# Sliding-window attention feeding a mixture of experts: reads of token rows ahead of weight loads and two groups ahead, constants and clearing spread over more attention units

## The chip, the cores and the metric

The kernel runs on one core of one Trainium2 chip. The metric is the device time of one execution in microseconds (us), a median of three runs. A core has five engines that work through their own instruction streams in order: TensorE (PE, matrix products; its weight loads are listed as PEld), VectorE (DVE), ScalarE (ACT), GpSimd (POOL) and SyncE (SP). SyncE does no arithmetic here: it issues nearly all loads, one after the other, and a load that must wait for something holds back every load behind it in the program. Sixteen DMA engines move the data.

## The reference

There are 4608 tokens (8 batches of 576) with 8 heads of 64. The first half is attention over a window of 128 positions with a bias that falls with the distance; the second half sends every token to the one of 8 experts whose logit is largest, and multiplies the expert's output by the softmax weight of that choice.

```python
def _attn_ref(q, k, v):                       # 8 batches, 8 heads, 576 positions, 64 per head
    scores = scale * np.matmul(q, k.transpose(0, 1, 3, 2))
    rel = pos[:, None] - pos[None, :]
    bias = slopes[:, None, None] * (-np.abs(rel).astype(np.float32))[None, :, :]
    mask = (rel >= 0) & (rel < 128)
    scores = np.where(mask, scores + bias[None], -1000000000.0)
    attn = softmax(scores)
    return np.matmul(attn, v)

def _moe_ref(x, w_gate, w1, w2):              # x: 4608 x 512; w1: 8 x 512 x 1024; w2: 8 x 1024 x 512
    logits = x @ w_gate
    expert_idx = np.argmax(logits, axis=1)
    gate_w = softmax(logits)[arange, expert_idx]
    for e in range(8):                        # tokens sorted by expert
        h = np.maximum(x_sorted[lo:hi] @ w1[e], 0.0)
        y_sorted[lo:hi] = h @ w2[e]
    return gate_w[:, None] * y_sorted[inv_perm]
```

(Softmax is written out in the original; it is shortened here.)

## The kernel before

**Attention.** The work is cut into 32 units (`NU`), one for each batch and pair of heads. Unit `u` computes scores on TensorE, exponentials on ScalarE, a product with a table of bias factors on VectorE (`factors`), and sums of overlapping blocks on GpSimd (`merge`, tile `mg`). TensorE then does `values` and `totals` of unit `u - 1`; `totals` reads `mg`. Once a batch is through, its gating is cut into "tasks" (logits, gate, rows, place, send), of which some are done in each later unit. A `send` scatters 128 finished rows of 514 numbers (512 values, the token's number, the gate weight) into the DRAM tensor `x_rows`, which holds a region for each expert. Each region's first 512 rows are cleared beforehand by `clear_rows`.

```python
later = [lambda: make_identity(nc, ident[:])]
def routing_constants():                        # all on GpSimd
    nc.gpsimd.memset(lt_strict[:], 1.0)
    nc.gpsimd.affine_select(lt_strict[:], lt_strict[:], compare_op=ALU.is_gt, ...)
    nc.gpsimd.memset(ones_sq[:], 1.0)
    ...                                         # zero_e, keep
later.append(routing_constants)

def iota(name, shape, pattern, base, mult, whole=False):
    t_i = consts.tile(shape, I32, name=name + "_i")
    later.append(lambda: nc.gpsimd.iota(t_i[:], ...))
    if whole:
        return t_i
    t_f = consts.tile(shape, F32, name=name)
    later.append(lambda: nc.gpsimd.tensor_copy(t_f[:], t_i[:]))
    return t_f
...                                             # first_w, region, thr, kx, tail, tok
        for u in range(NU + 1):
            b, hp = divmod(u, HP)
            slow = u < 7
            if u < NU:
                if u + HP < NU:
                    load_qk(u + HP)
                if hp == 1 and 1 < b + 1 < NB:
                    load_v(b + 1)
                if 0 < u <= E:
                    clear_rows(u - 1)
                ...
                scores(u)
                factors(u, 0)
            do(0 if slow else 1)                # so many tasks
            if u < NU:
                factors(u, 1)
                merge(u)
                if u + 1 < HP:
                    table(u + 1)
                if u == 2:
                    for make in later:
                        make()
                    start_routing()
            if u > 0:
                values(u - 1, 0)
                values(u - 1, 1)
                totals(u - 1)
                if hp == 0 and u < NU:
                    tasks += tasks_of(b - 1)
            do(0 if slow else 2 if len(tasks) < 14 else 3)
        do(len(tasks))
        last_tasks()
```

`last_tasks` does the gating of the last batch and, between its steps, the first 256 rows of expert 0 (`early`), whose outputs go through the attention's own tiles named `e` and are scattered to the output from there.

**Experts.** Fifteen groups follow: the other 256 rows of expert 0, then for each of experts 1 to 7 a full group of 512 rows, and after each of these a group of 128 rows (`x`) that did not fit. A full group is computed by a scheme of seven products for a 2x2 block product (`seven1`, `seven2`), the others plainly (`layer1`, `layer2`). `gather` reads a group's rows from `x_rows` into one of two `xg` buffers; `turn` transposes them on TensorE; `tokens` takes the row numbers out of `xg` for the scatter; the last step of a group scales its output by the gate weight, which it reads in `xg`.

```python
    def gather(g):
        n = g["n"]
        xg = g["xg"] = pools["x"].tile([P, NJ, RW], F32, name="xg")       # two buffers
        ...
            nc.sync.dma_start(xg[:, j0:j1, :], src[:, j0:j1, :])
    def layer2(g, j, ps, zo):
        ...
        nc.scalar.activation(zo, ps[:], AF.Copy, scale=g["xg"][:, j, Dm + 1 :])
        send_out(g, j, zo)
    ...
        g = groups[0]
        g["w1"], g["w2"] = expert_w.pop(0)      # loaded during attention
        get_w1(groups[1])
        gather(g)
        turn(g, range(g["n"]))
        for i, g in enumerate(groups):
            after = groups[i + 1 : i + 3] + [None, None]
            if after[0] is not None:
                gather(after[0])
                after[0]["w2"] = load_w2(after[0]["src"][1])
            ...                                 # layer 1: seven1 twice, or layer1
            tokens(g)
            if after[1] is not None:
                get_w1(after[1])
            if after[0] is not None:
                turn(after[0], range(after[0]["n"]))
                ...
            ...                                 # layer 2: seven2, or layer2
```

The pools of the expert stage are laid over those of attention, which are closed by then: `xg` (two buffers of 8 KB in each partition) falls on the buffers of k and v, and `weights1`, the second set of weight buffers, falls partly on the pool of `probs`, `e` and `mg`.

Of the kernel before, what the change touches and what calls it, by code (L numbers as in the profile page):

```python
# [21 lines left out]
def kernel(  # L22
# [47 lines left out]
    GT = KT + 1  # L70
    keep = consts.tile([P, E, GT + 1], F32, name="keep")

    def routing_constants():
        nc.gpsimd.memset(lt_strict[:], 1.0)
# [4 lines left out]
        nc.gpsimd.memset(ones_sq[:], 1.0)  # L79
        nc.gpsimd.memset(zero_e[:], 0.0)  # L80
        nc.gpsimd.memset(keep[:], 1.0)
        nc.gpsimd.memset(keep[:, :, 0:1], 0.0)

    later.append(routing_constants)

    def iota(name, shape, pattern, base, mult, whole=False):
        t_i = consts.tile(shape, I32, name=name + "_i")
        later.append(lambda: nc.gpsimd.iota(t_i[:], pattern=pattern, base=base, channel_multiplier=mult))
        if whole:
            return t_i  # L90
        t_f = consts.tile(shape, F32, name=name)
        later.append(lambda: nc.gpsimd.tensor_copy(t_f[:], t_i[:]))
        return t_f

    first_w = iota("first_w", [P, E], [[-1, E]], E, 0)
    region = iota("region", [P, E], [[N, E]], 0, 0)
# [17 lines left out]
    soon.append(lambda: nc.gpsimd.memset(zero_row[:], 0.0))  # L114
    soon.append(lambda: nc.gpsimd.memset(zero_row.bitcast(I32)[:, Dm : Dm + 1], 2 * N))

    def clear_rows(e):
        nc.sync.dma_start(
            x_d[e * N : e * N + CAP, :].rearrange("(j p) r -> p j r", p=P),
            zero_row[:, None, :].to_broadcast([P, NJ, RW]),  # L120
        )
# [59 lines left out]
            nc.vector.tensor_copy(early_n[:], rk[:, 0, GT:])  # L181

    def scatter(t, row):
        ins = nc.gpsimd.indirect_dma_start(  # L184
            out=x_d[:, :], out_offset=bass.IndirectOffsetOnAxis(ap=slots[:, t : t + 1], axis=0),
            in_=row, in_offset=None, bounds_check=E * N - 1, oob_is_err=False,
        )
        ins = getattr(ins, "ins", ins)
        tc.declare_no_dep(ins, group=f"rows_in{n_pass[0]}", reason="disjoint rows")
        tc.add_to_no_dep_group(f"rows_in{n_pass[0]}", ins)  # L190
# [239 lines left out]
            tc.add_to_no_dep_group(f"rows_out{n_pass[0]}", ins)  # L430

    def tokens(g):
        bits = g["xg"].bitcast(I32)[:, : g["n"], Dm]
        si = g["si"] = plain.tile([P, NJ], I32, name="si", bufs=2)[:, : g["n"]]
        if "mask" in g:
            nc.vector.tensor_tensor(si, bits, g["mask"][:, 0, :], op=ALU.bitwise_and)
            nc.vector.tensor_tensor(si, si, g["mask"][:, 1, :], op=ALU.bitwise_or)
        else:
            nc.vector.tensor_copy(si, bits)

    def turn(g, tiles, ps=None):

# [11 lines left out]
    def layer1(g, fb, ps):  # L454
        n = g["n"] * P
        if fb == 0:
            g["h"] = plain.tile([P, FB, EJ * P], F32, name="h2")
        for db in range(DB):
            nc.tensor.matmul(  # L459
                ps[:, :n], lhsT=g["w1"][:, db, fb * P : (fb + 1) * P], rhs=g["xT"][:, db, :n],  # L460
                start=(db == 0), stop=(db == DB - 1),
            )
        nc.scalar.activation(g["h"][:, fb, :n], ps[:, :n], AF.Relu)

    def layer2(g, j, ps, zo):
        for fb in range(FB):
            nc.tensor.matmul(  # L467
                ps[:], lhsT=g["h"][:, fb, j * P : (j + 1) * P], rhs=g["w2"][:, fb, :], start=(fb == 0),
                stop=(fb == FB - 1),
            )  # L470
        nc.scalar.activation(zo, ps[:], AF.Copy, scale=g["xg"][:, j, Dm + 1 :])  # L471
        send_out(g, j, zo)


# [22 lines left out]
    with tc.tile_pool(name="tab", bufs=1) as tab, \  # L497
# [257 lines left out]
        def last_tasks():  # L755
            g = early
            turns = [lambda j=j: turn(g, [j], sp_banks[j]) for j in range(EJ)]
            hid = [lambda fb=fb: layer1(g, fb, ps_m.tile([P, S - 2 * P], F32, name="m")) for fb in range(FB)]
            ts = tasks_of(NB - 1)
            more = {2: turns, 6: hid[:3], 8: hid[3:4], 9: hid[4:5], 10: hid[5:6], 11: hid[6:]}  # L760
            for i, task in enumerate(ts):
                task()
                for step in more.get(i + 1, ()):
                    step()
            extras(tab.tile([P, H, W // 2], F32, name="fac2").rearrange("p h c -> p (h c)"))
            tokens(g)
            for j in range(EJ):
                layer2(g, j, sp_banks[EJ + j], ex.tile([P, 2, W // 2], F32, name="e").rearrange("p a c -> p (a c)")[:, :Dm])

# [4 lines left out]
        load_v(1)  # L774
        tasks = []

        def do(n):
            for task in tasks[:n]:
                task()
            del tasks[:n]  # L780

        for u in range(NU + 1):
            b, hp = divmod(u, HP)

            slow = u < 7
            if u < NU:
                if u + HP < NU:
                    load_qk(u + HP)
                if hp == 1 and 1 < b + 1 < NB:
                    load_v(b + 1)  # L790
                if 0 < u <= E:
                    clear_rows(u - 1)
                if u == NU // 2:
                    expert_w[0] = load_w1(moe_w1[0]), load_w2(moe_w2[0])
                scores(u)
                factors(u, 0)
            do(0 if slow else 1)
            if u < NU:
                factors(u, 1)
                merge(u)  # L800
                if u + 1 < HP:
                    table(u + 1)
                if u == 2:
                    for make in later:
                        make()
                    start_routing()
            if u > 0:
                values(u - 1, 0)
                values(u - 1, 1)
                totals(u - 1)  # L810
                if hp == 0 and u < NU:
                    tasks += tasks_of(b - 1)
            do(0 if slow else 2 if len(tasks) < 14 else 3)
        do(len(tasks))
        last_tasks()

# [148 lines left out]
    def seven2(g, more):  # L965
# [17 lines left out]
        def weigh(th, dh, src):  # L983
            for i in range(2):
                j = 2 * th + i
                nc.scalar.activation(o[:, th, dh, i, :], src[:, i, :], AF.Copy, scale=g["xg"][:, j, Dm + 1 :])  # L986

        def post(n, ba, bb, bc):
            if n == 1:
# [56 lines left out]
    def experts(first):  # L1046
# [11 lines left out]
        if first:  # L1058
            g["w1"], g["w2"] = expert_w.pop(0)
        else:  # L1060
            get_w1(g)
        get_w1(groups[1])
        gather(g)
        if not first:
            g["w2"] = load_w2(g["src"][1])
            extras(pools["wk"].tile([P, FB, NJ * P], F32, name="h_sb").rearrange("p f n -> p (f n)"))
            run(w1_sums(g))
        turn(g, range(g["n"]))
        if not first:
            x_sums(g)  # L1070
        for i, g in enumerate(groups):
            after = groups[i + 1 : i + 3] + [None, None]
            full = [a for a in after if a is not None and a["n"] == NJ and "w1s" not in a]
            if after[0] is not None:
                gather(after[0])
                after[0]["w2"] = load_w2(after[0]["src"][1])
            if g["n"] == NJ:
                hidden(g)
                order = (1, 6, 7, 5, 2, 3, 4)
                ws = w2_sums(g)  # L1080
                seven1(g, 0, order, two_banks(3), temps(), {6: ws[:1], 7: ws[1:2], 5: ws[2:3], 3: ws[3:]})
# [8 lines left out]
            tokens(g)  # L1090
            if after[1] is not None:
                get_w1(after[1])
            if after[0] is not None:
                turn(after[0], range(after[0]["n"]))
                if after[0]["n"] == NJ:
                    x_sums(after[0])
            if i == 0 and first:
                count_in_range()
            if g["n"] == NJ:
                g["zo"] = pools["wk"].tile([P, NJ, Dm], F32, name="zo")  # L1100

                ws = w1_sums(full[0]) if full else []
# [8 lines left out]
    def plain_group(g):  # L1111
        get_w1(g)
        g["w2"] = load_w2(g["src"][1])
        gather(g)
        turn(g, range(g["n"]))
        for fb in range(FB):
            layer1(g, fb, bank(fb))
        tokens(g)
        plain_layer2(g)

    more = nc.values_load(n_more_i[0:1, 2:3], min_val=0, max_val=N * H + NX + EJ * P)
# [51 lines left out]
```

## Time and profile before

| | |
|---|---|
| time, median of 3 | 764.14 us (762.72 to 765.75) |
| span of the profiled execution | 763.8 us |
| TensorE busy | 704.8 us (92%) |
| VectorE busy | 368.6 us (48%) |
| ScalarE busy | 225.7 us (30%) |
| GpSimd busy | 184.2 us (24%) |
| DMA | 130.80 MB, mean 171 GB/s |

Attention with the gating of the last batch and the early rows of expert 0 ends near 247 us; the groups of experts run from there to about 752 us. "Busy" is the time in which an engine had an instruction under way. With TensorE busy for 92% of the span, the time that can be saved without changing the products lies in the remaining 8% and in the stretches in which its clock was low. A wait in the lists is written as "engine tile line <- what it waited for", then the sum in us, how many times, and the longest.

### The profile page before, as it was taken

Reading aid. Unit: us, or ns where it says so; the run is one execution under the profiler, and the core shown is the slowest. Engines: PE = TensorE matmul, PEld = TensorE weight load, DVE = VectorE, ACT = ScalarE, POOL = GpSimd, SP = SyncE. Lnnn points to the kernel's source line nnn. Section 1 sums busy time; section 2 is a strip of 40 time slices with the busy share of each in tenths; the row PEclk is TensorE's granted clock in tenths of the full one; section 3 lists DMA queues with packets and bytes.
Section 4 is the critical chain, followed back from the end, with each engine's and each line's share of the span. In section 5 each row is a group of like instructions: output and inputs, shape, how many; then the busy total and the mean of one; then the engine's idle time right before and its main releaser. Section 6 shows DMA issues by size and latency. Waiting matters only on the chain.

```text
span 763.8 us, 12630 instructions
## 1 busy us (share of the span) xinstructions
PE 704.8 (92%) x5158; PEld 566.2 (74%) x5158; DVE 368.6 (48%) x637; ACT 225.7 (30%) x538; POOL 184.2 (24%) x192
## 2 busy tenths in 40 slices
PE   5799899989999399999999999999999999999993
PEld 4576667667684277887888788788788978878891
DVE  8457677866654223532633544263453346235310
ACT  4555655545421021212213122221221213122120
POOL 5747766776541001011002001100200200020020
PEclk9899999989899599999999999999999999999997
DMA  9996668862121834209325720923663192275010
GB/s 335 371 374 214 213 225 314 257 188 91 54 84 42 315 111 151 98 27 332 112 111 178 288 110 28 340 94 111 221 246 110 54 359 64 95 280 189 1 56 7
DMA packets 54291, 130.80 MB, mean 171 GB/s; under 512 B 4175, under 2 KB 4175, under 8 KB 54224
## 3 DMA queue, kind: packets, MB, share of 16 engines
q1 hardware_dynamic: 47696, 110.97, 42.1%
q0 software_dynamic: 6000, 18.92, 6.5%
q8 instruction: 42, 0.69, 0.4%
q14 instruction: 25, 0.20, 0.1%
q10 hardware_dynamic: 528, 0.02, 0.0%
HBM read 102.55 MB, written 28.12 MB: 171 GB/s over the span
## 4 chain that ended last, share of the span: by engine, by line
PE 66%; issue 14%; DMA 6%; POOL 6%; DVE 5%; ACT 2%; SPq 0%; POOLq 0%; DVEq 0%
PE b L916 16%; PE a L916 11%; PE c L916 11%; PE a L467 5%; DMA xg<-x_rows 5%; PE m L625 5%; PE sp L580 5%; PE m L723 2%; PE sm L644 2%; POOL x_rows L184 2%; PE m L459 1%; PE a L459 1%; POOL mg L609 1%; DMA k_sb<-in_kT_dram 1%; POOL mg L606 1%
## 5 line engine op out<-in xcount | busy, mean ns | idle before, releaser
L422 POOL DMA_INDIRECT out_dram<-zo,si x28 | 29.5, 1053 | 326.1 <-ACT zo L986 321.8
L587 ACT ACTIVATE e<-sp 128x512 f32<-128x512 f32 x128 | 66.8, 600 | 44.7 <-PE sp L580 36.3
L606 POOL TENSOR_TENSOR mg<-probs 128x768 f32<-128x768 f32 x31 | 56.9, 1836 | 65.0 <-DVE probs L599 34.2
L625 PE MATMUL m<-probs,v_sb 128*64 128x256 f32 (+3 forms) x768 | 66.7, 322 | 1.2 <-DVE probs L594 0.8
L580 PE MATMUL sp<-q_sb,k_sb 64*64 64x192 f32 (+2 forms) x1152 | 57.1, 344 | 9.1 <-DMA k_sb<-in_kT_dram 9.0
L625 PEld LDWEIGHTS m<-probs,v_sb 128*64 128x64 f32 x768 | 49.9, 142 | 19.2 <-issue 4.7
L580 PEld LDWEIGHTS sp<-q_sb,k_sb 64*64 64x64 f32 x1152 | 48.5, 149 | 20.7 <-issue 9.8
L594 DVE TENSOR_TENSOR probs<-e,fac 128x1024 f32<-128x1024 f32 x32 | 40.5, 1267 | 42.0 <-ACT e L587 36.1
L467 PE MATMUL a<-w,h 128*128 128x512 f32 x128 | 56.3, 592 | 0.0
L986 ACT ACTIVATE zo<-zo,xg 128x256 f32<-128x256 f32 x42 | 19.1, 501 | 119.4 <-DVE zo L997 78.2
L916 PE MATMUL a<-xgT,w 128*128 128x256 f32 x224 | 53.0, 379 | 0.0
L916 PE MATMUL b<-xTs,w1s 128*128 128x256 f32 x224 | 52.9, 379 | 0.0
L916 PE MATMUL a<-w,h_sb 128*128 128x256 f32 x224 | 50.6, 379 | 0.0
L916 PE MATMUL b<-w2s,hs 128*128 128x256 f32 x224 | 50.6, 379 | 0.0
L916 PEld LDWEIGHTS a<-xgT,w 128*128 128x128 f32 x224 | 42.5, 190 | 8.7 <-issue 3.3
L184 POOL DMA_INDIRECT x_rows<-xs,slots x36 | 43.4, 1206 | 19.3 <-DVE xs L726 9.5
L916 PEld LDWEIGHTS b<-xTs,w1s 128*128 128x128 f32 x224 | 42.6, 190 | 5.8
L916 PEld LDWEIGHTS b<-w2s,hs 128*128 128x128 f32 x224 | 42.6, 190 | 5.8
L916 PEld LDWEIGHTS a<-w,h_sb 128*128 128x128 f32 x224 | 42.0, 190 | 5.4
L467 PEld LDWEIGHTS a<-w,h 128*128 128x128 f32 x128 | 23.7, 190 | 26.8 <-issue 26.8
L422 POOL DMA_INDIRECT out_dram<-zx,si x9 | 8.7, 972 | 139.7 <-ACT zx L471 139.7
L599 DVE TENSOR_TENSOR probs<-e,fac 128x1024 f32<-128x1024 f32 x32 | 40.5, 1264 | 2.0 <-ACT e L587 1.9
(212 smaller groups left out, 1178.2 us busy)
## 6 DMA issues: line engine op xcount, KB each, us to landing
w<-in_moe_w_dram SPq DMA_DIRECT2D x30, 2048.0 KB
q_sb<-in_qT_dram SPq DMA_DIRECT2D x32, 288.0 KB
k_sb<-in_kT_dram SPq DMA_DIRECT2D x32, 288.0 KB
x_rows<-zero_row SPq DMA_DIRECT2D x8, 1028.0 KB
xg<-x_rows SPq DMA_DIRECT2D x16, 514.0 KB
v_sb<-in_v_dram SPq DMA_DIRECT2D x8, 1024.0 KB
v_sb<-in_v_dram SPq DMA_DIRECT2D x8, 256.0 KB
xg<-x_rows SPq DMA_DIRECT2D x7, 257.0 KB
```

The source lines that it names most:

```text
L184: ins = nc.gpsimd.indirect_dma_start(out=x_d[:, :], out_offset=bass.IndirectOffsetOnAxis(ap=slots[:, t : t + 1], axis=0), in_=row, in_offs ...
L422: ins = nc.gpsimd.indirect_dma_start(out=out[:, :], out_offset=bass.IndirectOffsetOnAxis(ap=g["si"][:, j : j + 1], axis=0), in_=row, in_of ...
L459: nc.tensor.matmul(ps[:, :n], lhsT=g["w1"][:, db, fb * P : (fb + 1) * P], rhs=g["xT"][:, db, :n], start=(db == 0), stop=(db == DB - 1),)
L467: nc.tensor.matmul(ps[:], lhsT=g["h"][:, fb, j * P : (j + 1) * P], rhs=g["w2"][:, fb, :], start=(fb == 0), stop=(fb == FB - 1),)
L580: nc.tensor.matmul(sps[s][par][part * HALF : (part + 1) * HALF, c : c + n], lhsT=k_sb[u][half, k0 : k0 + HALF], rhs=q_sb[u][half, q0 : q0 ...
L587: nc.scalar.activation(exps[u][s][:, par, :], sps[s][par][:], AF.Exp, scale=D ** -0.5)
L594: nc.vector.tensor_tensor(to.rearrange("p a (j c) -> p a j c", c=2 * P), e.rearrange("p a (j c) -> p a j c", c=2 * P), fac[:, heads, None, ...
L599: nc.vector.tensor_tensor(to, e[:], fac2[:, heads, :], op=ALU.mult)
L606: eng.tensor_add(mg[:, :, : 3 * P].rearrange("p a (t c) -> p a t c", c=P), two[:, :, :, 0, :], two[:, :, :, 1, :],)
L625: nc.tensor.matmul(xp[par * HALF : (par + 1) * HALF, lo - q0 : hi - q0], lhsT=v_sb[b][:, j, h * D : (h + 1) * D], rhs=probs[u][:, par, c + ...
L916: nc.tensor.matmul(out_of[:, i, :], lhsT=lhs(i, k), rhs=rhs(k), start=(first and i == 0 and k == 0), stop=(k == nk - 1), skip_group_check= ...
L986: nc.scalar.activation(o[:, th, dh, i, :], src[:, i, :], AF.Copy, scale=g["xg"][:, j, Dm + 1 :])
```

## The change

It has four parts. (1) In the expert stage the rows of the first two groups are read ahead of the weight load that used to stand first on SyncE. (2) The rows of every further group are read two groups ahead instead of one; for that, `tokens` copies the gate weights into a small tile `gw` of their own as well, right after `turn`, so that an `xg` buffer is free once its rows are transposed and not only after the group's last product. (3) The constants for the routing are made in six portions, one in each of units 0 to 5 (the rest in unit 6), with the fills and conversions on VectorE and only the iotas and selects on GpSimd. (4) The eight clearings go to units 1, 2, 3, 4, 6, 7, 8 and 10 instead of 1 to 8; the tasks begin in unit 9 instead of 7, with up to four at the second place of a unit when 20 or more stand in line.

```diff
+    later += [
+        lambda: nc.vector.memset(lt_strict[:], 1.0),
+        lambda: nc.vector.memset(ones_sq[:], 1.0),
+        lambda: nc.vector.memset(zero_e[:], 0.0),
+    ]
     def iota(name, shape, pattern, base, mult, whole=False):
...
+        def make():
+            nc.gpsimd.iota(t_i[:], pattern=pattern, base=base, channel_multiplier=mult)
+            if not whole:
+                nc.vector.tensor_copy(t_f[:], t_i[:])
+        later.append(make)
...
+    def late_constants():
         nc.gpsimd.affine_select(lt_strict[:], ...)
+        nc.vector.memset(keep[:], 1.0)
+        nc.vector.memset(keep[:, :, 0:1], 0.0)
...
     def tokens(g):
...
+        nc.vector.tensor_copy(g["gw"][:, :n], g["xg"][:, :n, Dm + 1])
...
-        nc.scalar.activation(zo, ps[:], AF.Copy, scale=g["xg"][:, j, Dm + 1 :])
+        nc.scalar.activation(zo, ps[:], AF.Copy, scale=g["gw"][:, j : j + 1])
...
+        clears = [1 + 9 * i // (E - 1) for i in range(E)]
-            slow = u < 7
+            slow = u < clears[-1] - 1
-                if 0 < u <= E:
-                    clear_rows(u - 1)
+                if u in clears:
+                    clear_rows(clears.index(u))
-                if u == 2:
-                    for make in later:
+                if u < 6:
+                    for make in later[u::6]:
                         make()
+                if u == 6:
+                    late_constants()
                     start_routing()
-            do(0 if slow else 2 if len(tasks) < 14 else 3)
+            do(0 if slow else 2 if len(tasks) < 14 else 3 if len(tasks) < 20 else 4)
...
+        gather(g)
+        gather(groups[1])
         get_w1(groups[1])
-        gather(g)
...
         turn(g, range(g["n"]))
+        tokens(g)
         for i, g in enumerate(groups):
             after = groups[i + 1 : i + 3] + [None, None]
+            if after[1] is not None:
+                gather(after[1])
             if after[0] is not None:
-                gather(after[0])
                 after[0]["w2"] = load_w2(after[0]["src"][1])
...
-            tokens(g)
             if after[1] is not None:
                 get_w1(after[1])
             if after[0] is not None:
                 turn(after[0], range(after[0]["n"]))
+                tokens(after[0])
```

(The early group's `tokens` moves into `last_tasks`' steps after its `turn` in the same way; the scaling in `seven2` takes `gw` like that of `layer2`.)

More of the change, by code (lines that the diff above doesn't have):

```diff
@@ L71, with iota @@
     keep = consts.tile([P, E, GT + 1], F32, name="keep")
-    def routing_constants():
-        nc.gpsimd.memset(lt_strict[:], 1.0)
+    later += [
[3 more added lines that the diff above has]
+    ]
+    def iota(name, shape, pattern, base, mult, whole=False):
+        t_i = consts.tile(shape, I32, name=name + "_i")
+        t_f = None if whole else consts.tile(shape, F32, name=name)
+        def make():
[3 more added lines that the diff above has]
+        later.append(make)
+        return t_i if whole else t_f
+    def late_constants():
         nc.gpsimd.affine_select(
@@ L78, in routing_constants @@
         )
[L79 to L93, printed above, removed]
+        nc.vector.memset(keep[:], 1.0)
+        nc.vector.memset(keep[:, :, 0:1], 0.0)
     first_w = iota("first_w", [P, E], [[-1, E]], E, 0)
@@ L115 @@
     soon.append(lambda: nc.gpsimd.memset(zero_row.bitcast(I32)[:, Dm : Dm + 1], 2 * N))
+    cleared = []
     def clear_rows(e):
+        cleared.append(e)
         nc.sync.dma_start(
@@ L183, in scatter @@
     def scatter(t, row):
+        assert len(cleared) >= E
         ins = nc.gpsimd.indirect_dma_start(
@@ L432, in tokens @@
     def tokens(g):
-        bits = g["xg"].bitcast(I32)[:, : g["n"], Dm]
-        si = g["si"] = plain.tile([P, NJ], I32, name="si", bufs=2)[:, : g["n"]]
+        n = g["n"]
+        bits = g["xg"].bitcast(I32)[:, :n, Dm]
+        si = plain.tile([P, NJ], I32, name="si", bufs=2)
+        g["si"], g["gw"] = si, plain.tile([P, NJ], F32, name="gw", bufs=2)
         if "mask" in g:
-            nc.vector.tensor_tensor(si, bits, g["mask"][:, 0, :], op=ALU.bitwise_and)
-            nc.vector.tensor_tensor(si, si, g["mask"][:, 1, :], op=ALU.bitwise_or)
-        else:
-            nc.vector.tensor_copy(si, bits)
+            nc.vector.tensor_tensor(si[:, :n], bits, g["mask"][:, 0, :], op=ALU.bitwise_and)
+            nc.vector.tensor_tensor(si[:, :n], si[:, :n], g["mask"][:, 1, :], op=ALU.bitwise_or)
+        else:
+            nc.vector.tensor_copy(si[:, :n], bits)
+        nc.vector.tensor_copy(g["gw"][:, :n], g["xg"][:, :n, Dm + 1])
     def turn(g, tiles, ps=None):
@@ L758, in last_tasks @@
             hid = [lambda fb=fb: layer1(g, fb, ps_m.tile([P, S - 2 * P], F32, name="m")) for fb in range(FB)]
+            turns.append(lambda: tokens(g))
             ts = tasks_of(NB - 1)
@@ L985, in weigh @@
                 j = 2 * th + i
-                nc.scalar.activation(o[:, th, dh, i, :], src[:, i, :], AF.Copy, scale=g["xg"][:, j, Dm + 1 :])
+                nc.scalar.activation(o[:, th, dh, i, :], src[:, i, :], AF.Copy, scale=g["gw"][:, j : j + 1])
         def post(n, ba, bb, bc):
@@ L1089, in experts @@
                     layer1(g, fb, bank(fb))
-            tokens(g)
             if after[1] is not None:
@@ L1115, in plain_group @@
         turn(g, range(g["n"]))
+        tokens(g)
         for fb in range(FB):
             layer1(g, fb, bank(fb))
-        tokens(g)
         plain_layer2(g)
```

## The prediction

> **What bounds the kernel now.** I read the page's chain first, then the list of waits, then the timeline of the stretches that these two point at. The chain by engine:
>
> ```profile
> PE 66%; issue 14%; DMA 6%; POOL 6%; DVE 5%; ACT 2%; SPq 0%; POOLq 0%; DVEq 0%
> ```
>
> TensorE's products set the time (704.8 us busy of 763.8). No part of the change removes a product, so it can only win where TensorE stands or its clock is low. Here are the waits of TensorE that are not between its own steps (sum, times, longest):
>
> ```profile
> PE tp L450 <- DMA xg<-x_rows: 13.6, 1, 13.6
> ...
> PE sm L644 <- POOL mg L609: 10.8, 6, 3.3
> ...
> PE sp L580 <- DMA k_sb<-in_kT_dram: 9.0, 2, 5.0
> ...
> PE a L450 <- DMA xg<-x_rows: 4.9, 5, 1.8
> ```
>
> Two of the four are reads of rows (`xg`), one is GpSimd's `mg` that comes late, and the 9.0 us are the first loads of the kernel (until 4.97 and 11.81 us), which the change leaves alone. Why does the first `xg` come late? The DMA-issuing list of SyncE, then its timeline at the start of the expert stage:
>
> ```profile
> SPq L199 <- DMA out_dram<-e,si: 56.7, 1, 56.7
> ```
>
> ```profile
> 250.49 0.38 SPq L199 DMA_DIRECT2D w<-in_moe_w_dram  x1
> 251.09 1.57 SPq L1017 DMA_DIRECT2D xg<-x_rows  x3
> ...
> 260.14 1.94 PE L450 MATMUL tp<-ident,xg 128*128 128x128 f32 x8 [13.61 <-DMA xg<-x_rows]
> ```
>
> SyncE stood 56.7 us at the load of expert 1's w1 (L199), because that buffer lies over the pool of `e`, whose last scatter landed only at 250.25. The rows for which TensorE was waiting stood behind it in the program and were issued 0.6 us later, although their last scatter had been issued on GpSimd at 230.85. They then also landed behind 2 MB of weights, at 260.0.
>
> The third place is unit 3 of attention. GpSimd's timeline, and TensorE's beside it:
>
> ```profile
> 27.34 2.36 POOL L92 CAST thr<-thr_i 128x32 f32<-128x32 int32 x1
> 29.65 0.15 POOL L88 IOTA kx_i<- 128x32 int32 x1
> 29.86 1.13 POOL L92 CAST kx<-kx_i 128x32 f32<-128x32 int32 x1
> ...
> 32.19 1.79 POOL L606 TENSOR_TENSOR mg<-probs 128x768 f32<-128x768 f32 x1
> ```
>
> ```profile
> 26.22 1.54 PE L580 MATMUL sp<-q_sb,k_sb 64*64 64x192 f32 x36
> ...
> 34.45 1.28 PE L644 MATMUL sm<-mg,one_c 128*32 128x320 f32 x8 [3.34 <-POOL mg L609]
> 35.66 2.84 PE L580 MATMUL sp<-q_sb,k_sb 64*64 64x192 f32 x36
> ```
>
> All constants run on GpSimd from 24.98 to 32.2 us and stand ahead of unit 3's `mg`, which ends at 34.4. TensorE waits, and afterwards the same 36 score products take 2.84 us instead of 1.54: its clock has dropped.
>
> **What the Trainium skill says.** "TensorE: Matmul & The Clock Gate", section "What's actually happening": the clock halves after an idle window of about 3.4 us and comes back after as much busy time. The trace agrees: 2.84 against 1.54 us above, and a granted clock of 0.55 in 248 to 267 us. So a wait of several us costs up to 2 us more than itself. "DMA: Bandwidth & Descriptors", section "Queues, rings and completion order": each DMA engine takes up the descriptors of a ring in order. That fits the 8.91 us that the chain gives the first `xg` behind the weights, and it means that the order on SyncE decides, not the priority of the reader. "GPSIMD Engine Reference", section "3.1 Elementwise — side-by-side cycle accounting": an addition of two float tensors is 1.96 times slower there than on VectorE. Here `mg` takes 1.84 us on GpSimd and 0.96 on VectorE (the last unit), so GpSimd with `mg` and scatters is the engine to unload.
>
> **The change, part by part.**
>
> *Start of the expert stage.* The rows of groups 0 and 1 now go first. They need the last scatter (issued 230.85, so about 234) and a buffer that lies over k and v, whose last readers are done near 212; neither needs `e`. I take it that they land before TensorE ends the early rows' layer 2 at 246.5. The transposes can start when ScalarE has read that last PSUM bank (246.56 + 0.69 = 247.25). Then, all from the rows of before at full clock: transposes 1.0, wait for the copies 0.9, layer 1 of group 0 8 x 1.73 = 13.8, transposes of group 1 1.75, layer 2 2 x 6.87 = 13.7. Group 1's first product starts at 247.3 + 31.2 = 278.5 instead of 293.8: 15.3 us, of which 13.6 are the wait and the rest mostly the low clock behind it (the first of the eight layer-1 steps took 3.36 instead of 1.73). The weights of group 1 still leave at 250.4. 2 MB landed with the rows within 9.5 us before, so I put them at 258. VectorE then makes four sums of 1.22 us until 263, and the transposes of group 1 come at 263. That fits with nothing to spare, so I take off 0.3: **15.0 us**.
>
> *Rows two groups ahead.* SyncE's waits at L1017 for ScalarE (70.1 us at `zx`, 138.5 at `h`) are waits for a free `xg` buffer: the scaling reads the gate weight there. With `gw` the buffer is free after `turn`, a whole layer earlier, so the read is long done when it is needed. What TensorE gets is the 4.9 us of the list (five of the six remaining full groups, 0.7 to 1.8 each): **5.0 us** with the 0.3 of transposes behind them rounded down. The price is one more VectorE copy of 0.15 us in each group, beside TensorE's 6.87 us of layer 2.
>
> *Constants.* Unit 4 to 5 took 35.66 - 26.22 = 9.44 us and unit 5 to 6 took 6.36; units 2 to 4 and 6 took 4.03 each. So the stop costs 5.41 + 2.33 = 7.7 us. Against it: a conversion on VectorE now waits for an iota that stands behind `mg` on GpSimd, in units 0, 1, 2, 4 and 5. I followed one unit: scores end, exponentials 1 us per half, two factors of 1.22, `mg` 2.3 us. `mg` of unit u is ready about 7 us after its scores start and is needed at 7.4 (4.03 + 3.4). A conversion pushes the next factors by 0.3 to 1.4 us, which uses that slack up and stops TensorE by about 0.6 us two or three times. Net **6.0 us**.
>
> *Clearing and tasks.* The same bytes and tasks, later. DMA is full from 19 to 57 us (370 GB/s). Up to the last clearing it carries q and k of 15 units (0.59 MB each), four v (1.31) and eight clearings (1.05), 22.5 MB in all, so that one lands near 62 us. Unit 10 should start near 56 (unit 2 at 18.15, seven units of 4.03 and 1.3 of stops, then five tasks of some 4 us in unit 9), and its first send stands behind its `mg`, at 63: no or little wait. Counting tasks by the two rules, units 7 and 8 lose three and four, unit 9 has five, and from unit 25 on both orders are the same. The worst heap of sends between two `mg` (five of them; TensorE then waited 2.81 us and ran at low clock at 99.63 us) goes from unit 13 to unit 21. I take off **0.5**.
>
> Sum: 15.0 + 5.0 + 6.0 - 0.5 = 25.5, so 764.1 - 25.5 = 738.6 us.
>
> **Rivals.** *The rows still wait for `e`:* if the pools of attention are released as one, the first rows leave at 250.4 too, only ahead of the weights. They would land some 6 us sooner than 260.0, and the weights as much later. Against it speaks that only the weights' pool lies over `e`; what speaks for it is that the issue log shows the rows straight behind the weights, so their own condition is not seen. Then about 748. *A new bound at the same place:* group 1's weights, sums and copies (258, 263) come later than TensorE's 263, for instance because w2 shares the bandwidth; each us is lost one for one, up to about 5: 744. *Attention gives its part back:* VectorE is held by GpSimd in five units and the later, denser tasks pile scatters (1 to 2 us each) before `mg`; one wait of 3 us with low clock costs 5. In the worst case the 5.5 are gone: 744; with luck in the heaps (10.8 us of waits for `mg` in all, 3.3 of it the constants) it gains 4 more: 735.
>
> **Range and chances.** The steady part is nearly sure, the expert start probable, the attention part loose by about 4 either way. One rival alone leaves 744 to 748; two together are needed for more. That gives 731 to 748. The limit of 2% is 748.9 us: faster by over 2% 0.88, within 2% 0.11, slower 0.01.
>
> **What would show it.** Right: no wait of TensorE for `xg` over 1 us; the first rows issued near 230 us on the new clock and group 1's first product some 31 us after the early rows end; the gap between the starts of units 4 and 5 near 4 to 5 us with products of 1.54; SyncE's wait for ScalarE at the gather gone. Wrong: rows issued after the scatter of `e`; VectorE waiting for the sums' weights beyond layer 1 of group 0; `sm` waits for `mg` above 10 us in sum or new low-clock units between 40 and 170 us; scatters waiting for a clearing.

## The result, and the profile after

The changed kernel takes 743.49 us (median of four runs, 742.47 to 744.34) against 764.65 (762.72 to 765.75) for the kernel before in the same session: a ratio of 0.9725, 95% interval 0.9699 to 0.9751. It is 21 us faster, where 25.5 were predicted (738.6, range 731 to 748). The profiled span goes from 763.8 to 740.7 us, the mean granted clock from 0.967 to 0.982. These two executions lie 23.1 us apart, 1.9 more than the medians, because they took 765.55 and 742.47 us.

The chain of work that ended last, by engine, and the line of busy times of TensorE:

```profile
PE 72%; issue 13%; POOL 7%; DVE 4%; ACT 1%; DMA 1%; POOLq 0%; DVEq 0%
...
PE 698.2 (94%) x5158; PEld 562.2 (76%) x5158; DVE 377.3 (51%) x663; ACT 225.7 (30%) x538; POOL 181.4 (24%) x182
```

The chain's share of DMA has fallen from 6% to 1%, that of GpSimd has risen from 6% to 7%. The list of TensorE's waits says the same (sum in us, times, longest):

```profile
PE sm L656 <- POOL mg L621: 14.5, 7, 3.7
PE sp L592 <- DMA k_sb<-in_kT_dram: 7.4, 2, 5.0
...
PE tp L462 <- ACT e L483: 0.8, 1, 0.8
```

Both lines for `xg` (13.6 and 4.9 us before) are gone. The wait for `mg`, which the constants and clearing were to shorten, has grown from 10.8 to 14.5 us. The expert stage, first in SyncE's list of issues, then in TensorE's timeline, then in VectorE's (start, duration, what; in brackets the idle time before it and what ended that):

```profile
232.46 1.40 SPq L1032 DMA_DIRECT2D xg<-x_rows  x3
248.48 0.37 SPq L207 DMA_DIRECT2D w<-in_moe_w_dram  x1
```

```profile
245.45 1.09 PE L462 MATMUL tp<-ident,xg 128*128 128x128 f32 x8 [0.78 <-ACT e L483]
247.49 1.96 PE L471 MATMUL a<-xT,w 128*128 128x256 f32 x8 [0.94 <-DVE gw L451]
...
261.38 1.04 PE L462 MATMUL tp<-ident,xg 128*128 128x128 f32 x8
...
276.86 1.89 PE L931 MATMUL a<-xgT,w 128*128 128x256 f32 x8
```

```profile
256.44 1.22 DVE L893 TENSOR_TENSOR w1s<-w 128x1024 f32<-128x1024 f32 x1 [8.95 <-DMA w<-in_moe_w_dram]
...
259.98 1.22 DVE L894 TENSOR_TENSOR w1s<-w,w1s 128x1024 f32<-128x1024 f32 x1
```

The rows leave at 232.46 instead of 251.09 and do not wait for `e`; the weights still leave when `e` is scattered. TensorE's only stop is the 0.8 us for ScalarE's read of the last PSUM bank and 0.9 for the copies. The weights' sums end at 261.2, just before the transposes of group 1.

Cut into the three stages of the prediction, from the two traces: the early rows end at 244.7 instead of 246.5 (1.85 us); from there group 1's first product comes 15.1 us sooner (it starts at 276.86 instead of 293.78, less those 1.85); from that product to the end it is 463.8 instead of 470.0 us (6.2). Attention, put at 5.5 us, is the stage that did not deliver. The next section asks why.

### The profile page after: what moved, and what is told of

Read it like the earlier page. It is cut to its first block, busy times and chain, and to the rows that moved or that the text cites. A ratio compares the mean times of both kernels' runs of the same rounds, so it can differ in the third digit from the quotient of the medians.

```text
span 740.7 us, 12619 instructions
## 1 busy us (share of the span) xinstructions
PE 698.2 (94%) x5158; PEld 562.2 (76%) x5158; DVE 377.3 (51%) x663; ACT 225.7 (30%) x538; POOL 181.4 (24%) x182
## 4 chain that ended last, share of the span: by engine, by line
PE 72%; issue 13%; POOL 7%; DVE 4%; ACT 1%; DMA 1%; POOLq 0%; DVEq 0%
PE b L931 17%; PE a L931 11%; PE c L931 11%; PE a L479 6%; PE m L637 4%; PE sp L592 4%; PE a L471 3%; PE b L471 3%; POOL x_rows L192 2%; PE m L471 2%; PE sp L479 2%; PE sm L656 2%; PE c L471 2%; PE m L735 2%; POOL mg L618 2%
## 5 line engine op out<-in xcount | busy, mean ns | idle before, releaser
L618 POOL TENSOR_TENSOR mg<-probs 128x768 f32<-128x768 f32 x31 | 56.4, 1820 | 66.6 <-DVE probs L611 33.6
L637 PE MATMUL m<-probs,v_sb 128*64 128x256 f32 (+3 forms) x768 | 64.1, 315 | 1.5 <-DVE xs L738 1.1
L637 PEld LDWEIGHTS m<-probs,v_sb 128*64 128x64 f32 x768 | 48.2, 137 | 18.2 <-issue 2.6
L606 DVE TENSOR_TENSOR probs<-e,fac 128x1024 f32<-128x1024 f32 x32 | 41.9, 1309 | 26.8 <-ACT e L599 25.0
L1001 ACT ACTIVATE zo<-zo,gw 128x256 f32<-128x256 f32 x42 | 19.1, 501 | 119.4 <-DVE zo L1012 78.2
L611 DVE TENSOR_TENSOR probs<-e,fac 128x1024 f32<-128x1024 f32 x32 | 42.7, 1334 | 0.2 <-ACT e L599 0.2
L961 DVE TENSOR_TENSOR u<-b,p 128x512 f32<-128x512 f32 x14 | 9.7, 692 | 56.4 <-PE b L931 56.4
```

Of the source, the lines that this page charges most:

```text
L606: nc.vector.tensor_tensor(to.rearrange("p a (j c) -> p a j c", c=2 * P), e.rearrange("p a (j c) -> p a j c", c=2 * P), fac[:, heads, None, ...
L611: nc.vector.tensor_tensor(to, e[:], fac2[:, heads, :], op=ALU.mult)
L618: eng.tensor_add(mg[:, :, : 3 * P].rearrange("p a (t c) -> p a t c", c=P), two[:, :, :, 0, :], two[:, :, :, 1, :],)
L637: nc.tensor.matmul(xp[par * HALF : (par + 1) * HALF, lo - q0 : hi - q0], lhsT=v_sb[b][:, j, h * D : (h + 1) * D], rhs=probs[u][:, par, c + ...
```

## The experiments

All ratios are to the kernel before, on the same chip. Two changed kernels are compared by medians that can come from different chips; the kernel before had medians of 763.57 to 764.65 us there, so about 1 us of such a difference says nothing. The table, from one execution of each kernel, gives the start of the scores of some units (us). "Experts only" has parts 1 and 2 of the change, "constants only" part 3, both described below.

| unit | before | experts only | constants only | half clearing | after | sums on VectorE |
|---|---|---|---|---|---|---|
| 4 | 26.22 | 24.38 | 25.10 | 25.11 | 25.08 | 25.19 |
| 5 | 35.66 | 34.25 | 31.04 | 31.04 | 31.02 | 29.23 |
| 9 | 59.47 | 58.06 | 55.16 | 55.16 | 50.67 | 45.36 |
| 12 | 78.70 | 77.29 | 77.75 | 76.25 | 69.83 | |
| 14 | 89.77 | 88.36 | 89.71 | 87.31 | 87.31 | 77.67 |
| 23 | 147.92 | 146.43 | 149.04 | 145.44 | 147.69 | |
| 31 | 204.25 | 202.53 | 206.20 | 202.50 | 202.14 | 180.70 |

**Rows behind the weights.** Is it the order on SyncE that gave the 15 us? The changed kernel, with that order alone put back:

```diff
+        get_w1(groups[1])
         gather(g)
         gather(groups[1])
-        get_w1(groups[1])
```

> The kernel after with one line moved: the load of expert 1's w1 stands ahead of the first two reads of rows on SyncE again. My theory (the order on SyncE alone was worth 15 us): the first rows leave only when the scatter of e has landed, near 248 us, TensorE waits 13 to 14 us for them, and the time goes from 743.5 to 757 to 759. The rival (the rows would have to wait for e anyway, or the pause was mostly hidden): no more than 6 us slower, 749 or less.

Measured: 758.45 us (757.39 to 759.38), ratio 0.9931 [0.9910, 0.9953], 15.0 us above the changed kernel, as the theory had it. This kernel's line in TensorE's waits, and SyncE's timeline:

```profile
PE tp L462 <- DMA xg<-x_rows: 13.2, 1, 13.2
```

```profile
249.06 0.38 SPq L207 DMA_DIRECT2D w<-in_moe_w_dram  x1
249.66 12.04 SPq L1032 DMA_DIRECT2D xg<-x_rows  x4
```

The rows stand behind the weights again, and group 1's first product is at 291.99. The same loads with the same conditions, in another order on one engine, are worth 15.0 us.

**One group ahead.** Part 2 has two pieces: reading two groups ahead, and the copy of the gate weights that frees the buffer early. This run keeps the copy and reads only one group ahead:

```diff
-            if after[1] is not None:
-                gather(after[1])
+            if i > 0 and after[0] is not None:
+                gather(after[0])
```

> The kernel after with every further group read one group ahead again, but with the gate weights still copied (the buffer still comes free after the transposes). My theory (part 2 wins about 6 us, and most of it comes from the second half of a full group's rows, which are read during the 7 us of the small group's layer 1): TensorE waits again 0.7 to 2 us at the transposes of five or six full groups, 747 to 749.5. The rival (the copy of the gate weights alone is what counts, since it frees the buffer): no wait, 743 to 744.5.

Measured: 744.35 us (743.70 to 744.92), ratio 0.9756 [0.9732, 0.9780]; no wait of TensorE for `xg`; from group 1's first product to the end 463.7 us against 463.8. The distance is worth nothing that can be measured. The steady part comes with the copy, as the rival said: with it SyncE is no longer held at the gather by ScalarE. (The distance without the copy was not run.)

**Parts 1 and 2 alone.** The kernel before with the expert stage of the changed one; constants, clearing and tasks as before. As a diff against the changed kernel:

```diff
-                if u < 6:
-                    for make in later[u::6]:
+                if u == 2:
+                    for make in later:
                         make()
 ...                                    # constants filled and converted on GpSimd again
-            slow = u < clears[-1] - 1
+            slow = u < 7
 ...                                    # clearings in units 1 to 8, up to three tasks
```

> The kernel before with parts 1 and 2 alone (both orders of reads, the copied gate weights). My theory (constants, clearing and tasks together are worth 2 us or less): 743.5 to 745.5. The prediction's own sums (attention 5.5): 748 to 749.

Measured: 741.67 us (740.42 to 743.70), ratio 0.9713 [0.9688, 0.9738], no slower than the whole change. So parts 3 and 4 together give nothing. The 1.85 us between the two traces are not theirs either: this kernel, with attention as before, is 1.84 us ahead at unit 4 and 1.72 at unit 31. Its first loads came sooner. Unit 1 started at 11.81 us in the recorded profile of before and between 10.07 and 11.13 in the other kernels that load in the same order.

**Constants only.** The kernel before with part 3:

```diff
-                if u == 2:
-                    for make in later:
+                if u < 6:
+                    for make in later[u::6]:
                         make()
+                if u == 6:
+                    late_constants()
 ...                                    # fills and conversions on VectorE
```

> The kernel before with part 3 alone (constants in portions, conversions on VectorE). My theory now (the 7.7 us of the stop are removed, but VectorE waits for iotas behind mg in units 4 to 6 and about half is given back): unit 4 to 5 about 6 us instead of 9.44, a new wait of 2 to 3 us of the totals for mg in unit 6 or 7, unit 8 starts 2 to 4 us sooner, time 760.5 to 762.5. The rival, the prediction's own figure (net 6 us): 758.5. If nothing of it reaches the end: 764.6.

Measured: 766.02 us (762.91 to 768.87), ratio 1.0031 [1.0019, 1.0044]. Both forecasts of a gain missed: it is a little slower than before. The table shows how. By unit 9 it is 2.9 us ahead of "experts only", by unit 12 nothing is left, at unit 31 it is 3.7 behind (in the execution shown, its slowest). What comes in between is the first send, in this kernel's timeline of GpSimd:

```profile
57.28 0.18 POOL L721 COPY xs<-tok_i 128x2 int32<-128x2 int32 x1
61.47 1.16 POOL L188 DMA_INDIRECT x_rows<-xs,slots  x1 [4.00 <-DVE xs L730]
62.63 0.19 POOL L721 COPY xs<-tok_i 128x2 int32<-128x2 int32 x1
62.78 1.82 POOL L610 TENSOR_TENSOR mg<-probs 128x768 f32<-128x768 f32 x1
```

The send could not leave although its row (`xs`) was ready, and the next `mg` stood behind it. What it awaited I took to be the last clearing, issued at 45.94; the line names VectorE, which had finished this row by 56.4. That could be tested.

**Half the clearing.** The same kernel, but only rows 256 to 511 of each region are cleared, half the bytes (the smallest of these regions gets 462 tokens, so with this input the first 256 rows are filled anyway; for every input it would not do):

```diff
-            x_d[e * N : e * N + CAP, :].rearrange("(j p) r -> p j r", p=P),
-            zero_row[:, None, :].to_broadcast([P, NJ, RW]),
+            x_d[e * N + CAP // 2 : e * N + CAP, :].rearrange("(j p) r -> p j r", p=P),
+            zero_row[:, None, :].to_broadcast([P, NJ // 2, RW]),
```

> The kernel before with part 3 alone, and the clearings cut to rows 256 to 511 of each region (half the bytes; the first 256 rows of every region are overwritten with this input, whose smallest group has 462 rows, so the output stays the reference's, but the kernel would not be right for every input). My theory (constants alone win about 3 us up to unit 9, and the first send then stands at 61.47 us until the last clearing has landed and holds back the sums mg behind it): the first send starts before 58.5 us, units 10 to 13 start 2 to 4 us sooner than with whole clearings, time 760 to 763. The rival (the sends' own heap or VectorE's waits are what gives it back): units 12 to 14 as before, 765 to 767.

Measured: 765.09 us (762.27 to 770.36), ratio 1.0016 [0.9999, 1.0032]. The send left at 59.54 instead of 61.47, the idle time before it fell from 4.00 to 2.06 us, and unit 14 came 2.4 us sooner. So the clearing does hold the send. The remaining 2 us are not its: here the last clearing was issued at 42.00 and no recorded one took over 10.2 us to land. At unit 31 the traces are 3.7 us apart, but that of "constants only" is its slowest execution (768.87 us, against 763.62 here); the medians are 0.9 apart. The time missed its expectation, and of the 5.41 + 2.33 us that the constants cost, nothing arrives at the end. The clearing is one of the takers in this kernel, not the only one.

**Tasks and clearing as before.** The changed kernel with part 4 undone:

```diff
-            slow = u < clears[-1] - 1
+            slow = u < 7
-                if u in clears:
-                    clear_rows(clears.index(u))
+                if 0 < u <= E:
+                    clear_rows(u - 1)
-            do(0 if slow else 2 if len(tasks) < 14 else 3 if len(tasks) < 20 else 4)
+            do(0 if slow else 2 if len(tasks) < 14 else 3)
```

> The kernel after with part 4 undone (clearings in units 1 to 8, tasks from unit 7, two or three at the second place). My theory (the later, denser tasks heap up sends before mg in units 11 and 21 and give back what the constants won): attention ends 2 to 4 us sooner, 739.5 to 741.5. The rival (part 4 is what kept DMA and first units free, worth 2 us or more): 745.5 or more. The prediction's own figure (costs 0.5): 743.

Measured: 744.79 us (742.95 to 746.04), ratio 0.9757 [0.9728, 0.9786]; the intervals overlap, so part 4 is worth about 1 us or nothing. It was expected to run at 739.5 to 741.5. The changed kernel is 7.5 us ahead of "experts only" at unit 12, but part of that lead is tasks put off, and it is lost where they are done: units 12 and 22 take 10.33 and 10.80 us. Before the stop in unit 22, five sends hold GpSimd from 133.34 to 141.12 ahead of `mg`, which is what the prediction called the heap, and put in unit 21. The changed kernel's last lines of GpSimd in it, then TensorE's stops for such heaps:

```profile
138.85 0.99 POOL L192 DMA_INDIRECT x_rows<-xs,slots  x1 [0.16 <-issue]
140.15 0.97 POOL L192 DMA_INDIRECT x_rows<-xs,slots  x1 [0.30 <-issue]
141.13 1.82 POOL L618 TENSOR_TENSOR mg<-probs 128x768 f32<-128x768 f32 x1
```

```profile
77.31 0.73 PE L656 MATMUL sm<-mg,one_c 128*32 128x320 f32 x8 [3.07 <-POOL mg L621]
...
144.41 1.28 PE L656 MATMUL sm<-mg,one_c 128*32 128x320 f32 x8 [2.89 <-POOL mg L621]
...
191.68 1.28 PE L656 MATMUL sm<-mg,one_c 128*32 128x320 f32 x8 [3.66 <-POOL mg L621]
```

The kernel before had three such stops, of 2.81, 2.05 and 1.79 us.

**Why is each delay on GpSimd so costly?** The timelines of the changed kernel in units 6 and 7, VectorE, then GpSimd, then TensorE:

```profile
38.88 0.17 DVE L86 CAST region<-region_i 128x8 f32<-128x8 int32 x1 [2.54 <-POOL region_i L84]
...
41.60 1.74 DVE L145 COPY sel<-region 1x8 f32<-1x8 f32 x1
43.26 1.21 DVE L606 TENSOR_TENSOR probs<-e,fac 128x1024 f32<-128x1024 f32 x1
44.39 1.20 DVE L611 TENSOR_TENSOR probs<-e,fac 128x1024 f32<-128x1024 f32 x1
```

```profile
38.30 0.46 POOL L621 TENSOR_TENSOR mg<-probs 128x128 f32<-128x128 f32 x1
...
41.49 1.82 POOL L618 TENSOR_TENSOR mg<-probs 128x768 f32<-128x768 f32 x1 [2.65 <-DVE keep L96]
43.27 2.65 POOL L621 TENSOR_TENSOR mg<-probs 128x128 f32<-128x128 f32 x1
```

```profile
45.97 0.73 PE L656 MATMUL sm<-mg,one_c 128*32 128x320 f32 x8 [2.72 <-POOL mg L621]
```

A conversion of 0.17 us waits 2.54 us for an iota that GpSimd reaches only behind `mg`. Then a copy of eight numbers on VectorE takes 1.74 us: it ends with the `mg` addition that GpSimd began 0.11 us before it. And the small `mg` addition, 0.46 us when VectorE is idle, takes 2.65: it ends 0.3 us after the two factors that VectorE began at the same moment. The two engines look as if one holds the other up. The Trainium skill, "SBUF — State Buffer", section "Who interferes with whom", says so of VectorE's products: a VectorE instruction with two SBUF inputs contends with a GpSimd instruction that reads SBUF. (The copy has one input; why it waited is not shown.) VectorE can be the one that loses even when it starts first (here a send held GpSimd until 74.02):

```profile
73.65 3.30 DVE L611 TENSOR_TENSOR probs<-e,fac 128x1024 f32<-128x1024 f32 x1
```

```profile
74.03 1.82 POOL L618 TENSOR_TENSOR mg<-probs 128x768 f32<-128x768 f32 x1
```

If this contention is the limit, the work of `mg` belongs on VectorE even though it is the busier of the two.

**Sums on VectorE.** The changed kernel with one line altered, so that GpSimd keeps only sends, small copies, iotas and selects:

```diff
-            eng = nc.vector if u == NU - 1 else nc.gpsimd
+            eng = nc.vector
```

> The kernel after with merge (the sums mg) on VectorE in all units, not only in the last. My theory (GpSimd and VectorE hold each other up in the first units, and heaps of sends on GpSimd make mg late): the waits of the totals for mg (14.5 us in sum) fall below 3 us, attention ends 8 to 14 us sooner, 730 to 736. The rival (VectorE, 51% busy but over 60% in attention, becomes the bound with 1.24 us more in each unit): the score products wait for the factors instead, 742 to 750.

Measured: 721.97 us (721.10 to 723.07), ratio 0.9458 [0.9432, 0.9484], 21.5 us faster than the changed kernel and more than expected. No wait for `mg` is left, and the clock is 0.993. The groups of VectorE's products between 4 and 240 us (busy us, mean ns of one, then idle time before them):

```profile
L606 DVE TENSOR_TENSOR probs<-e,fac 128x1024 f32<-128x1024 f32 x32 | 39.1, 1223 | 11.8 <-ACT e L599 11.6
L611 DVE TENSOR_TENSOR probs<-e,fac 128x1024 f32<-128x1024 f32 x32 | 39.0, 1220 | 0.0
L618 DVE TENSOR_TENSOR mg<-probs 128x768 f32<-128x768 f32 x32 | 30.7, 958 | 1.9
L621 DVE TENSOR_TENSOR mg<-probs 128x128 f32<-128x128 f32 x32 | 9.1, 284 | 0.0
```

In the changed kernel the first two had 1309 and 1334 ns, 6.4 us of busy time more in all. VectorE took over 31 times 1.24 us of sums and yet TensorE waits less.

**Useless additions on GpSimd.** Was it the shared ports, or only that `mg` no longer stands behind sends? This kernel is the last one with two additions of the old sizes put back on GpSimd in units 4 to 30. They read a constant table and write a scratch tile that nothing reads:

```diff
+            if 4 <= u < NU - 1:
+                nc.gpsimd.tensor_add(shade[:, :, : 3 * P], fac2[:, 0:2, : 3 * P], fac2[:, 2:4, : 3 * P])
+                nc.gpsimd.tensor_add(shade[:, :, 3 * P : S - P], fac2[:, 0:2, :HALF], fac2[:, 2:4, :HALF])
```

> The kernel after with merge on VectorE, and in units 4 to 30 two additions of the same sizes left on GpSimd as well, of constant tables into a scratch tile that nothing reads; sends stay on GpSimd behind them. It adds work that the reference doesn't have. If GpSimd's additions and VectorE's two-input operations keep each other off the memory (my theory for half of the gain of 21.5 us): VectorE's factors grow from 1.2-1.3 to over 1.5 us and the time rises to 728 to 738. If only the place of mg in GpSimd's line counted: factors as before, 721 to 724.

Measured: 764.25 us (761.15 to 768.52), ratio 1.0012 [0.9991, 1.0033], 42 us slower than without them and more than either theory asked. The groups of the same stretch, line numbers shifted by two:

```profile
L613 DVE TENSOR_TENSOR probs<-e,fac 128x1024 f32<-128x1024 f32 x32 | 53.2, 1662 | 2.1 <-ACT e L601 2.1
...
L620 DVE TENSOR_TENSOR mg<-probs 128x768 f32<-128x768 f32 x32 | 41.4, 1293 | 1.9
...
L626 POOL TENSOR_TENSOR h<-fac 128x128 f32<-128x128 f32 x27 | 27.9, 1033 | 0.0
L623 DVE TENSOR_TENSOR mg<-probs 128x128 f32<-128x128 f32 x32 | 17.6, 550 | 0.0
```

Nothing waits for their results, but VectorE's instructions beside them are longer: 1220 to 1662 ns, 958 to 1293, 284 to 550. In busy time, with L608 (39.1 to 40.2), the four groups grow by 14.2 + 10.7 + 8.5 + 1.1 = 34.5 us. That agrees with the skill's sentence on two SBUF inputs, and the useless additions themselves took 1033 ns for 128x128 in the mean. The loss reaches TensorE through VectorE: its waits for VectorE from 4 to 240 us sum to 29.1 us, against 5.1 without the additions (leaving out `gw`), and none names GpSimd. The three largest:

```profile
PE m L740 <- DVE rs_all L702: 5.1, 1, 5.1
PE m L642 <- DVE rs_all L702: 4.8, 1, 4.8
PE sm L661 <- DVE mg L623: 4.7, 3, 2.0
```

How the rest of the 42 us divides, between the lower clock (0.969 against 0.993) and sends that now stand behind the additions, was not separated. Nor does this run say how much of the 21.5 us was the ports: it has more contention than the changed kernel, where the factors were only 6.4 us longer in sum. Keeping `mg` on GpSimd but ahead of the sends, which would have told, was not run.

**Sums on VectorE without parts 3 and 4.** Two kernels: the one before with the altered line alone, and with parts 1 and 2 as well.

> The kernel before with merge on VectorE in all units and nothing else. My theory (in the kernel before, too, what holds up TensorE in attention is mg behind other work of GpSimd, the constants among it, so one move does what parts 3 and 4 were meant to do and more): 740 to 744, with no wait of the totals for mg. The rival (it works only together with the constants and tasks of the change): 750 or more.

> The kernel before with parts 1 and 2 and with merge on VectorE in all units: the faster kernel of the last set without parts 3 and 4. My theory (with mg off GpSimd, neither constants nor heaps of sends there hold up TensorE, so parts 3 and 4 have nothing left to win): 720 to 724.5. The rival (parts 3 and 4 win their 5 us once GpSimd is out of the way): 726 to 728.

The altered line alone: 747.62 us (745.88 to 750.55), ratio 0.9804 [0.9768, 0.9840], 17 us from one line, between the two expectations; the early rows end at 226.9 instead of 246.5, the expert stage still starts with 13.4 us of waiting. The stop between units 4 and 5 has gone (4.03 us) though the constants still stand on GpSimd: it cost only because `mg` stood behind them. With parts 1 and 2: 723.52 us (721.21 to 724.21), ratio 0.9466 [0.9439, 0.9494], within its expectation and not to be told from the 721.97 with all four parts. Parts 3 and 4 find nothing to win here either.

**A faster start.** What is left at the beginning is the wait for the first loads. The kernel with the sums on VectorE, with q and k of unit 1 loaded ahead of v:

```diff
         load_qk(0)
+        load_qk(1)
         load_v(0)
-        for u in range(1, HP):
+        for u in range(2, HP):
```

> The kernel after with merge on VectorE in all units, and q and k of unit 1 loaded ahead of v of batch 0. The first waits of TensorE (7.7 us in sum: until 4.97 and again before unit 1) are waits for q and k behind 1.3 MB of v that is needed only after unit 1's scores. Theory: unit 1 starts near 8 us instead of 10.5, time 719 to 720.5. The rival (v then lands late and values of unit 0 wait the same time): 721.5 to 722.5.

Measured: 719.34 us (719.17 to 719.44), ratio 0.9419 [0.9398, 0.9441]: the fastest of all, 24 us below the changed kernel and 44 below the one before (763.65 on the same chip). Unit 1 starts at 8.24 instead of 10.52. Its busy line, with TensorE at 96% and GpSimd at 14%:

```profile
PE 686.9 (96%) x5158; PEld 557.2 (78%) x5158; DVE 391.3 (55%) x725; ACT 225.5 (31%) x538; POOL 101.8 (14%) x120
```

## Why the prediction was right, and where it was not

*Start of the expert stage, 15.0 us: right, by its own steps.* Measured 15.1, and 15.0 when the order alone was put back. The rows did leave near 230 (232.46), not after the scatter of `e`, so the first rival falls. The weights' sums began at 256.4 and ended at 261.2, where 258 and 263 were put (the early rows ended 1.85 us sooner); the fit was as tight as expected and held, so the second rival falls too. From the end of the early rows to group 1's first product it took 32.2 us, where the working had 32.0 (246.5 to 278.5). One reading was off without touching the sum: 3.36 us is the length of the first layer-1 step and 1.73 the distance between later ones, whose length is 1.89.

*Rows two groups ahead, 5.0 us: the size about right (6.2), the mechanism right in one half.* What freed the loads was the `gw` copy, which the prediction named. The distance in the heading contributes nothing. (The five waits were 0.52 to 1.77 us each, not 0.7 to 1.8; their sum was right.)

*Constants, "Net 6.0 us", less 0.5 for clearing and tasks: this is the step that failed.* Measured 1.85 us in the two traces and nothing once the chance in the first loads is taken out. Against the medians the sum missed by 4.3 us: attention fell 5.5 short, and the reads came 1.3 better than put. The stop itself was read rightly and did shrink: unit 4 to 5 took 5.94 us instead of 9.44, where "near 4 to 5 us" was to be seen. What was wrong is the sum behind it. It took a gain in unit 4 as a gain at the end, as if the stops behind it stayed as they were. Two terms were mis-sized. The waits behind conversions, put at "about 0.6 us two or three times", were 0.52, 1.50 and 2.72 us in units 3, 4 and 7, 4.7 in sum. The heaps of sends, for which with the later clearing 0.5 was taken off, made stops of 3.1, 2.9 and 3.7 us in units 12, 22 and 29, 9.6 in sum where the kernel before had 6.7. The two excesses, about 3 us each, are the size of what is missing. Part 4 alone did not make the heaps: such stops sum to 10.2 us with it undone too, and to 7.0 in "experts only", so the heaps grew once the constants had moved. Why they did is only in part shown. Waits for `mg` "above 10 us in sum" were the sign given for being wrong, and the sum rose to 14.5. One cause is the clearing, where it keeps its old place: with constants alone the first send waited for it, and half the clearing let it go 1.9 us sooner. In the changed kernel that send left right behind its `mg`, as the prediction had it:

```profile
66.59 1.15 POOL L192 DMA_INDIRECT x_rows<-xs,slots  x1 [0.18 <-POOL mg L621]
```

The third rival, that attention gives its part back, is what happened: it named 744, and 743.49 was measured. It got the carriers right (conversions behind GpSimd, denser scatters ahead of `mg`) but not the remedy. The prediction compared 1.84 with 0.96 us for `mg` on the two engines and concluded that GpSimd was to be unloaded; it did not ask whether the additions on GpSimd also lengthen VectorE's own. Putting them on VectorE won 17 to 21.5 us in the stage in which parts 3 and 4 won nothing.

What stays open: how much of the waits behind conversions and heaps, and of the gain with the sums on VectorE, goes to the shared ports and how much to the order of work on GpSimd.

## What to carry to other kernels

On an engine that issues loads in order, sort them by when their conditions are met, and free a buffer early (here with a copy of 0.16 us) before reading further ahead: the order gave 15 us, the freed buffer 6, the distance nothing. A stop removed early is a gain only if the stops behind it do not grow, so follow the gain through to the last unit before adding it to the sum. And elementwise work given to GpSimd beside a busy VectorE is not free help: measure the VectorE instructions beside it, and try the move back.

## What the runs showed of the hardware that was not expected

- A GpSimd addition of 128x128 took 0.45 us with VectorE idle and 1.45 or 2.65 us beside VectorE's products; in the other direction a VectorE copy of eight numbers took 1.74 us, and a product of 128x1024 took 1662 ns in the mean instead of 1220.
- Two additions for each unit that nothing waits for made the kernel 42 us slower (721.97 to 764.25).
- The first loads of the kernel landed at different times in the profiles: unit 1 started between 10.07 and 11.81 us with the same order of loads. A difference of 1.8 us at the end of attention between two traces is no gain until it is placed.
